# Letting ready large products go ahead of small ones in a planned TensorE order

## The chip, the core and the metric

The kernel runs on one core of a Trainium2 chip. The metric is the device time of one execution in microseconds (us): the median of several runs. Lower is better. TensorE (PE) multiplies, VectorE (DVE), ScalarE (ACT) and GpSimd (POOL) do the element work, SyncE (SP) and the other queues start DMAs. PE's clock has two levels, 1.2 and 2.4 GHz; the profile gives the granted clock as 0.50 or 1.00.

## The reference

```python
def _attn_ref(q, k, v, beta):                       # 4 x 8 heads, 768 tokens, 48 wide
    k_n = k / (norm(k) + 1e-06)
    state = 0                                       # 48 x 48 for each head
    for t in range(768):
        y[t] = q[t] @ state
        state = state + beta[t] * outer(k_n[t], v[t] - k_n[t] @ state)
    return y

x = attn_out as 3072 tokens x 384
h = x @ w_in;  x = (h * sigmoid(1.702 * h)) @ w_out          # 384 -> 2048 -> 384
h = relu(x @ w2_in);  out = (h * h) @ w2_out                 # 384 -> 2048 -> 384
```

## The kernel before

The recurrence is cut into 12 chunks of 64 tokens. Inside a chunk a triangular system is solved (loops on POOL over tiles `U` and `gu`, transposes on DVE), and the chunks follow one another through the state in `ws`. Two chunks give the 512 columns of one tile of the first feed-forward layer, so that this layer starts when chunk 0 is done and runs while the next chunks are computed. The second layer follows, with no small products in it.

PE does two kinds of work here:

- **Large products.** A *group* is three matmuls that follow each other (high by high, high by low, low by high half of an exact split): an *h group* multiplies one third of `x` by a slice of the weights `wi` into PSUM tile `h`; a *z group* multiplies the activated slice `ghi`/`glo` by `wo` into one of three PSUM tiles `z`. Step f of a tile (f = 0 to 15) has three h groups and, later, three z groups. In the first tile steps 0 to 7 are done in two halves of 256 columns, half a (chunk 0) and half b (chunk 1); all other groups are 512 columns wide. Also large: *A* (`a<-kq`, 64x128 x8, the Gram matrices of a chunk) and *Y* (`a<-pqa,ws` and `a<-pqb,ws`, the chunk's output).
- **Small products** of the recurrence: *merge* (`a<-Td,G` and `a<-kT_sb`, 32x16 x64), *W* (`a<-v_sb,Td`, 32x48 x16), *G* (`a<-ws,G`), *S* (`a<-ws,k_sb`, the new state), *X* (`a<-ws,kT_sb`, the state times the keys).

The chain of a chunk is X, subtraction from `v_sb` on DVE, transposes, merge, `Td` on DVE, W, copy to `ws` on ACT, G, subtraction on DVE, W, copy, Y and S, and then X of the next chunk.

The order on every engine is written by a planner, the class `Program`, before the kernel runs. Each operation is added with its queue (or a choice of queues), costs and the tiles it reads and writes; its place in the source, less or more an offset, is its *rank*. `flush` then steps through a time of its own: of the engine that is free first it takes the ready operation with the lowest rank (`n = r[0][1]`, r being a heap of the ready ones), unless an urgent one is due soon, and issues it. Engines work strictly through what is issued to them in this order. A matmul operation carries `cold`, a pair of its cost at the low clock and a count of columns, which the helper `mms` (L275 is its matmul line) sets from a density: 1.0 for groups and A, 0.65 for Y, 0.1 to 0.33 for the small products.

The weights of both layers come as 64-bit floats and are split into two halves for exact products: `split_w` does this on ACT and DVE, and its last subtraction (to `wi_lo` or `wo_lo`) goes to POOL or DVE, whichever the planner has free.

Of the kernel before, what the change touches and what calls it, by code (L numbers as in the profile page):

```python
# [29 lines left out]
TUNE = dict(  # L30
    fused=4,
    warm=(10, 6),
    blocks=(0, 1, 2, 3),
    ja=4,
    depth=2,
    half=8,
    slack=0.0,
    first=2,
# [11 lines left out]
class Program:  # L50
# [8 lines left out]
    def __init__(self, queues):  # L59
        self.queues = queues  # L60
        self.ops = []
        self.writer, self.readers = {}, {}
        self.free = {q: 0.0 for q in queues}
        self.dma_free = 0.0
        self.urgent = False
        self.columns = {}

    def add(self, queue, cost, fn, reads=(), writes=(), early=0, nbytes=0, after=(), cold=None):
        n = len(self.ops)
        deps = set(after)  # L70
        for k in reads:
            if k in self.writer:
                deps.add(self.writer[k])
        for k in writes:
            if k in self.writer:
                deps.add(self.writer[k])
            deps.update(self.readers.get(k, ()))
        for k in reads:
            self.readers.setdefault(k, []).append(n)
        for k in writes:  # L80
            self.writer[k], self.readers[k] = n, []
        queue = (queue,) if isinstance(queue, str) else queue
        cost = cost if isinstance(cost, tuple) else (cost,)
        self.ops.append([queue, cost, fn, deps, n - early, nbytes, None, self.urgent, cold])

    def flush(self):
        left, users, todo = {}, {}, 0
        future = {q: [] for q in self.queues}
        ready = {q: [] for q in self.queues}
        ops = self.ops  # L90

        def arrive(n):
            queue, cost, fn, deps, rank, nbytes, end, urgent, cold = ops[n]
            t = max([ops[d][6] + (self.OWN_LATENCY if ops[d][0] == queue else self.LATENCY) for d in deps], default=0.0)
            for q in queue:
                heapq.heappush(future[q], (t, rank, n))

        for n, op in enumerate(ops):
            if op[6] is None:
                todo += 1  # L100
                wait = [d for d in op[3] if ops[d][6] is None]
                left[n] = len(wait)
                for d in wait:
                    users.setdefault(d, []).append(n)
        for n in left:
            if not left[n]:
                arrive(n)
        done = set()
        while todo:
            best = None  # L110
            for q in self.queues:
                f, r = future[q], ready[q]
                while r and r[0][1] in done:
                    heapq.heappop(r)
                while f and f[0][2] in done:
                    heapq.heappop(f)
                if r or f:
                    t = self.free[q] if r else max(self.free[q], f[0][0])
                    if best is None or t < best[0]:
                        best = (t, q)  # L120
            t, q = best
            f, r = future[q], ready[q]
            while f and f[0][0] <= t:
                x = heapq.heappop(f)
                heapq.heappush(r, (x[1], x[2]))
            while r[0][1] in done:
                heapq.heappop(r)
                if not r:
                    break
            if not r:  # L130
                continue
            n = r[0][1]
            queue, cost, fn, deps, rank, nbytes, end, urgent, cold = ops[n]
            c = cost[queue.index(q)]
            if cold:
                tick = t // self.TICK
                if self.columns.get(tick - 1, 0) < self.WARM_COLUMNS:
                    c = cold[0]
            if not urgent:
                soon = min((x[0] for x in f if ops[x[2]][7] and x[1] < rank and x[2] not in done), default=None)  # L140
                if soon is not None and soon < t + c - TUNE["slack"]:
                    self.free[q] = soon
                    continue
            heapq.heappop(r)
            if cold:
                self.columns[tick] = self.columns.get(tick, 0) + cold[1]
            self.free[q] = t + c
            if nbytes:
                start = max(t + self.DMA_START, self.dma_free)
                self.dma_free = start + nbytes / self.DMA_RATE  # L150
                ops[n][6] = self.dma_free + self.DMA_END
            else:
                ops[n][6] = t + c
            done.add(n)
            todo -= 1
            fn(self.queues[q])
            for u in users.get(n, ()):
                left[u] -= 1
                if not left[u]:
                    arrive(u)  # L160
# [798 lines left out]
```

## Time and profile before

| | |
|---|---|
| median of 3 runs | 1097.75 us (1096.6 to 1100.5) |
| the profiled execution | 1099.22 us, of it 1097.5 us from the first to the last instruction |
| PE busy | 1045.0 us, 95% |
| DVE, ACT, POOL busy | 590.7, 529.8, 339.3 us |
| mean granted clock | 0.960 |
| first tile's steps | about 60 to 222 us of the span |

How to read the rows further down: in the page's strip of 40 slices each digit is a tenth, and 9 is 90% or more. A row of windows has the stretch, then busy time and number of instructions of PE, of the weight loads PEld, of DVE, ACT and POOL, then the granted clock, the share of DMA time and GB/s. A row of the timeline has start, duration, engine, line, operation, tiles, form, count, and in brackets the idle time before it with what ended it. Matmuls overlap in the pipeline, so that the time a group takes is read from the start of its first matmul to the start of what follows, not from the durations. An fp32 matmul of the small kind shows as two records (x32 for 16).

### The profile page before, as it was taken

What the parts mean: (1) busy time and instruction counts of PE and PEld (TensorE: products, weight loads), DVE (VectorE), ACT (ScalarE), POOL (GpSimd) and SP (SyncE); (2) the same over time, 40 slices, a digit from 0 to 9 for tenths busy, and PEclk for the clock granted to TensorE, in tenths of its full rate; (3) what the DMA queues carried; (4) which work ended last, traced back from release to release, by engine and by line L of the source; (5) the groups of instructions that cost most, each with busy time, mean ns of one, the idle gap of its engine ahead of it and who ended that gap; (6) DMA issues with size and microseconds to landing.
All of it is one profiled execution on the core that took longest, in us unless ns stands there. A gap on an engine that the chain in (4) does not pass through costs nothing.

```text
span 1097.5 us, 23999 instructions
## 1 busy us (share of the span) xinstructions
PE 1045.0 (95%) x9900; PEld 847.5 (77%) x9900; DVE 590.7 (54%) x1116; ACT 529.8 (48%) x1088; POOL 339.3 (31%) x679
## 2 busy tenths in 40 slices
PE   5789898989999999999999989999999999999998
PEld 3788787767768776777787866788888888888886
DVE  6788765673636455554644599734333343333332
ACT  4676656555454546454633656633334343333323
POOL 1355351568655573738280044200000000000000
PEclk7688868999999999999999999999999999999999
DMA  7365442223122213222110466401001010000000
GB/s 226 94 180 155 119 130 80 73 69 92 37 76 66 75 41 93 70 69 63 59 34 1 135 176 169 129 1 30 29 1 58 1 58 1 1 30 1 30 1 29
DMA packets 43981, 76.32 MB, mean 70 GB/s; under 512 B 6624, under 2 KB 19552, under 8 KB 43872
## 3 DMA queue, kind: packets, MB, share of 16 engines
q1 hardware_dynamic: 43776, 74.75, 23.1%
q8 instruction: 77, 1.26, 0.5%
q14 instruction: 32, 0.26, 0.1%
q10 hardware_dynamic: 96, 0.05, 0.0%
HBM read 64.16 MB, written 9.44 MB: 67 GB/s over the span
## 4 chain that ended last, share of the span: by engine, by line
PE 68%; DVE 15%; ACT 7%; issue 4%; POOL 4%; DMA 2%; ACTq 0%; SPq 0%; DVEq 0%; POOLq 0%
PE h L275 29%; PE z L275 28%; PE a L275 11%; DVE c L262 3%; ACT G L248 2%; DVE kT_sb L268 2%; DVE glo L258 2%; DVE g L265 1%; DVE c L265 1%; DVE gu L268 1%; POOL tmpp L519 1%; POOL U L522 1%; DMA raw<-in_w_out 1%; DVE v_sb L258 1%; ACT gu L243 1%
## 5 line engine op out<-in xcount | busy, mean ns | idle before, releaser
L243 ACT ACTIVATE g<-h 128x512 f32<-128x512 f32 (+1 forms) x200 | 115.8, 580 | 272.7 <-PE h L275 270.1
L275 PE MATMUL z<-glo,wo_hi 128*128 128x512 f32 (+1 forms) x600 | 233.0, 388 | 6.6 <-DVE glo L258 6.4
L275 PE MATMUL z<-ghi,wo_hi 128*128 128x512 f32 (+1 forms) x600 | 233.1, 388 | 0.6 <-ACT ghi L243 0.5
L275 PE MATMUL z<-ghi,wo_lo 128*128 128x512 f32 (+1 forms) x600 | 230.5, 384 | 0.0
L258 DVE TENSOR_TENSOR glo<-g,ghi 128x512 fp32r<-128x512 f32 (+1 forms) x200 | 137.2, 686 | 102.6 <-ACT ghi L243 102.0
L243 ACT ACTIVATE ghi<-g 128x512 fp32r<-128x512 f32 (+1 forms) x200 | 122.5, 614 | 132.6 <-DVE g L265 65.8
L258 DVE TENSOR_TENSOR g<-g,h 128x512 f32<-128x512 f32 x96 | 66.0, 688 | 172.3 <-ACT g L243 172.2
L275 PE MATMUL h<-x_hi,wi_hi 128*128 128x512 f32 (+1 forms) x312 | 133.5, 428 | 11.0 <-DVE g L265 7.8
L275 PEld LDWEIGHTS z<-glo,wo_hi 128*128 128x128 f32 x600 | 114.7, 191 | 35.8 <-DVE glo L258 14.1
L519 POOL TENSOR_TENSOR tmpp<-U,gu 128x126 f32<-128x126 f32 (+22 forms) x248 | 110.2, 445 | 93.7 <-DVE U L262 75.0
L275 PEld LDWEIGHTS z<-ghi,wo_hi 128*128 128x128 f32 x600 | 114.7, 191 | 25.0 <-ACT ghi L243 1.7
L275 PEld LDWEIGHTS z<-ghi,wo_lo 128*128 128x128 f32 x600 | 114.7, 191 | 21.4
L275 PE MATMUL h<-x_lo,wi_hi 128*128 128x512 f32 (+1 forms) x312 | 122.0, 391 | 3.7 <-DVE x_lo L258 3.6
L265 DVE SCALAR_TENSOR_TENSOR g<-g,h 128x512 f32<-128x512 f32 (+1 forms) x104 | 66.5, 640 | 104.5 <-ACT g L243 104.2
L275 PE MATMUL h<-x_hi,wi_lo 128*128 128x512 f32 (+1 forms) x312 | 121.0, 388 | 0.0
L275 PE MATMUL h<-x_hi,vi_hi 128*128 128x512 f32 x288 | 112.2, 390 | 0.8 <-PE h L275 0.8
L275 PE MATMUL h<-x_hi,vi_lo 128*128 128x512 f32 x288 | 112.1, 389 | 0.0
L522 POOL TENSOR_TENSOR U<-U,tmpp 128x126 f32<-128x126 f32 (+22 forms) x248 | 104.9, 423 | 21.2 <-DVE U L262 2.0
L275 PEld LDWEIGHTS h<-x_hi,wi_hi 128*128 128x128 f32 x312 | 61.5, 197 | 35.3 <-DVE g L265 16.3
L275 PEld LDWEIGHTS h<-x_lo,wi_hi 128*128 128x128 f32 x312 | 62.3, 200 | 12.7 <-DVE x_lo L258 6.0
L275 PEld LDWEIGHTS h<-x_hi,wi_lo 128*128 128x128 f32 x312 | 62.4, 200 | 11.2
L262 DVE TENSOR_SCALAR c<-raw 128x384 uint16<-128x384 uint16 x128 | 64.8, 545 | 5.9 <-DMA raw<-in_w_in 2.9
(117 smaller groups left out, 1457.6 us busy)
## 6 DMA issues: line engine op xcount, KB each, us to landing
raw<-in_w_in SPq DMA_DIRECT2D x32, 384.0 KB, 3.7
raw<-in_w_out SPq DMA_DIRECT2D x32, 384.0 KB, 3.5
kq<-in_kq SPq DMA_DIRECT2D x44, 256.0 KB, 3.0
kT_sb<-in_kq SPq DMA_DIRECT2D x11, 512.0 KB, 4.2
k_sb<-in_kt SPq DMA_DIRECT2D x12, 384.0 KB, 4.3
v_sb<-in_vt SPq DMA_DIRECT2D x12, 384.0 KB, 3.1
xf_sb<-zd SPq DMA_DIRECT2D x18, 256.0 KB, 2.7
out<-zs SPq DMA_DIRECT2D x18, 256.0 KB, 2.0
```

The source lines that it names most:

```text
L243: pg.add("act", c_act(n), lambda e: e.activation(**kw), reads, writes, early)
L248: e.activation(out=out, in_=in_, func=AF.Copy)
L258: pg.add(queue, cost, lambda e: e.tensor_tensor(out=out, in0=in0, in1=in1, op=op), reads, writes, early)
L262: pg.add("dve", c_dve(n, True), lambda e: e.tensor_scalar(**kw), reads, writes, early)
L265: pg.add("dve", c_dve(n), lambda e: e.scalar_tensor_tensor(**kw), reads, writes, early)
L268: pg.add("dve", c_dve(n), lambda e: e.transpose(out=out, in_=in_), reads, writes)
L275: e.matmul(out=out, lhsT=lhsT, rhs=rhs, start=start, stop=stop)
L519: e.tensor_tensor(out=t, in0=U[:, lo:hi, j:j + 1].to_broadcast(shape), in1=gu[:, j + 1:, j:j + 1].rearrange("p i o -> p o i").to_broadcast ...
L522: e.tensor_tensor(out=U[:, lo:hi, j + 1:], in0=U[:, lo:hi, j + 1:], in1=t, op=ALU.add)
```

## The change

`Program` gets a second way to choose on PE. When the lowest-ranked ready operation is small, the planner's time is at most 220, and 6 us of it have passed since the last long row of large products ended, the ready large operation of the lowest rank is taken instead. A row counts as long when large operations have followed each other without a gap for 4 us of planned time.

```diff
+    burst=(6, 4, 220),
...
+        self.run = self.run_end = self.burst_end = 0.0
...
+    def large(self, n):
+        cost, cold = self.ops[n][1], self.ops[n][8]
+        return cold is None or cold[1] > 1400 * cost[0]
+
+    def large_first(self, r, t, done):
+
+        pause, length, until = TUNE["burst"]
+        if t > until or t < self.burst_end + pause or self.large(r[0][1]):
+            return 0
+        ready = [(x, k) for k, x in enumerate(r) if x[1] not in done and self.large(x[1])]
+        return min(ready)[1] if ready else 0
...
-            n = r[0][1]
+            k = self.large_first(r, t, done) if q == "pe" else 0
+            n = r[k][1]
...
-            if not urgent:
+            if not urgent and not k:
...
-            heapq.heappop(r)
+            if k:
+                r[k] = r[-1]
+                r.pop()
+                heapq.heapify(r)
+            else:
+                heapq.heappop(r)
+            if q == "pe":
+                self.run = (self.run if self.large(n) and t < self.run_end + 0.3 else 0.0) + (c if self.large(n) else 0.0)
+                self.run_end = t + c
+                if self.run >= TUNE["burst"][1]:
+                    self.burst_end = t + c
```

No instruction is added or dropped. The order is the same up to the merge that the trace of before shows at 77.75 us, and PE's is the same again from 558 us. Lines after the class stand 25 lower, so that the matmul line L275 is L300 in the changed kernel. What moves is seen at three places on PE.

First, the second merge of chunk 1 (`a_74<-kT_sb`), in step 5 of half a. Before, it stands right behind the first h group of the step, then A and both W, then large groups:

```order
L275 MATMUL h_68<-x_hi_80,wi_hi 128x256
L275 MATMUL h_68<-x_lo_81,wi_hi 128x256
L275 MATMUL h_68<-x_hi_80,wi_lo 128x256
L275 MATMUL a_74<-kT_sb 32x16 x64
L275 MATMUL a_73<-kq_100 64x128 x8
L275 MATMUL a_74<-v_sb,Td_112 32x48 x16
L275 MATMUL a_72<-v_sb,Td_112 32x48 x16
L275 MATMUL h_68<-x_hi_80,wi_hi 128x256
```

In the change the same merge follows A and five groups, of which these are the last two, and the first W comes one h group later:

```order
L300 MATMUL z_70<-ghi_84,wo_hi 128x256
L300 MATMUL z_70<-glo_86,wo_hi 128x256
L300 MATMUL z_70<-ghi_84,wo_lo 128x256
L300 MATMUL z_71<-ghi_84,wo_hi 128x256
L300 MATMUL z_71<-glo_86,wo_hi 128x256
L300 MATMUL z_71<-ghi_84,wo_lo 128x256
L300 MATMUL a_74<-kT_sb 32x16 x64
L300 MATMUL h_67<-x_hi_80,wi_hi 128x256
L300 MATMUL h_67<-x_lo_81,wi_hi 128x256
L300 MATMUL h_67<-x_hi_80,wi_lo 128x256
L300 MATMUL a_74<-v_sb,Td_112 32x48 x16
```

So merge and A have changed places, five groups have gone ahead of the merge, and the second W (`a_72`) comes after five groups more. Further on in this chunk the first h group of step 7 has moved ahead of the third W.

Second, chunk 2 after its merges, in steps 4 to 8 of half b. Before, two W stand after three groups, then two groups, a G, a group, a G, and so on:

```order
L275 MATMUL z_69<-ghi_84,wo_hi 128x256
L275 MATMUL z_69<-glo_86,wo_hi 128x256
L275 MATMUL z_69<-ghi_84,wo_lo 128x256
L275 MATMUL a_74<-v_sb,Td_111 32x48 x16
L275 MATMUL a_72<-v_sb,Td_111 32x48 x16
L275 MATMUL h_67<-x_hi_80,wi_hi 128x256
L275 MATMUL h_67<-x_lo_81,wi_hi 128x256
L275 MATMUL h_67<-x_hi_80,wi_lo 128x256
L275 MATMUL z_70<-ghi_84,wo_hi 128x256
L275 MATMUL z_70<-glo_86,wo_hi 128x256
L275 MATMUL z_70<-ghi_84,wo_lo 128x256
L275 MATMUL a_73<-ws_95,G_105 32x48
```

In the change eleven groups stand in one row between the merge and the first W. These are the last two, and what follows them:

```order
L300 MATMUL h_68<-x_hi_80,wi_hi 128x256
L300 MATMUL h_68<-x_lo_81,wi_hi 128x256
L300 MATMUL h_68<-x_hi_80,wi_lo 128x256
L300 MATMUL z_71<-ghi_84,wo_hi 128x256
L300 MATMUL z_71<-glo_86,wo_hi 128x256
L300 MATMUL z_71<-ghi_84,wo_lo 128x256
L300 MATMUL a_74<-v_sb,Td_111 32x48 x16
L300 MATMUL h_67<-x_hi_80,wi_hi 128x512
L300 MATMUL h_67<-x_lo_81,wi_hi 128x512
L300 MATMUL h_67<-x_hi_80,wi_lo 128x512
L300 MATMUL a_72<-v_sb,Td_111 32x48 x16
```

The W and G of chunk 2 have moved 10 to 14 operations back; behind the second W follow six more groups before the first G.

Third, A and the merges of chunk 3, in steps 10 and 11. Before, both stand ahead of the last h group of step 10 and all z groups of step 9:

```order
L275 MATMUL a_73<-kq_99 64x128 x8
L275 MATMUL a_74<-Td_112,G_106 32x16 x64
L275 MATMUL h_67<-x_hi_80,wi_hi 128x512
L275 MATMUL h_67<-x_lo_81,wi_hi 128x512
L275 MATMUL h_67<-x_hi_80,wi_lo 128x512
L275 MATMUL z_69<-ghi_85,wo_hi 128x512
```

In the change that h group and the three z groups come first, and one h group of step 11 stands between A and the merge:

```order
L300 MATMUL z_71<-ghi_85,wo_hi 128x512
L300 MATMUL z_71<-glo_87,wo_hi 128x512
L300 MATMUL z_71<-ghi_85,wo_lo 128x512
L300 MATMUL a_73<-kq_99 64x128 x8
L300 MATMUL h_68<-x_hi_80,wi_hi 128x512
L300 MATMUL h_68<-x_lo_81,wi_hi 128x512
L300 MATMUL h_68<-x_hi_80,wi_lo 128x512
L300 MATMUL a_74<-Td_112,G_106 32x16 x64
```

So five groups have gone ahead of the merge. The planner's time shifts with all this, and so the other engines' orders change too: among others, six subtractions to `wi_lo` and `wo_lo` go from POOL to DVE.

## Rows read from the trace of the kernel before

**Rows 1.** The page, granted clock of PE in 40 slices.

```profile
PEclk7688868999999999999999999999999999999999
```

**Rows 2.** Windows, cut where the granted clock changes.

```profile
core 0: us, PE busy (x) PEld busy (x) DVE busy (x) ACT busy (x) POOL busy (x), PEclk, DMA share, GB/s
...
82.10:88.90 6.80, 6.01 (x70) 5.70 (x65) 5.19 (x11) 4.02 (x11) 2.28 (x2) 0.50 0.54 174
...
106.00:109.40 3.40, 3.40 (x17) 3.40 (x18) 3.22 (x8) 2.23 (x7) 2.83 (x7) 0.50 1.03 333
...
123.00:126.50 3.50, 3.27 (x17) 2.98 (x16) 3.50 (x9) 0.84 (x3) 0.00 (x0) 0.51 0.42 112
...
133.30:153.80 20.50, 20.50 (x290) 18.57 (x290) 12.10 (x30) 9.45 (x22) 8.78 (x21) 0.50 0.41 115
...
170.80:177.70 6.90, 5.74 (x148) 4.44 (x144) 4.35 (x7) 3.55 (x9) 0.53 (x1) 0.51 0.16 42
177.70:230.00 52.30, 52.30 (x761) 42.20 (x761) 27.43 (x52) 32.67 (x76) 26.91 (x55) 1.00 0.30 90
230.00:242.00 12.00, 9.12 (x38) 6.31 (x37) 11.59 (x25) 4.29 (x7) 6.10 (x13) 1.00 0.01 1
```

**Rows 3.** Timeline of PE, in the stretch at the low clock.

```profile
140.91 1.49 PE L275 MATMUL a<-ws,G 32*32 32x48 f32 x32
142.33 0.58 PE L275 MATMUL z<-ghi,wo_hi 128*128 128x256 f32 x1
...
143.13 0.41 PE L275 MATMUL h<-x_hi,wi_hi 128*128 128x256 f32 x1
...
143.77 0.41 PE L275 MATMUL z<-ghi,wo_hi 128*128 128x256 f32 x1
...
145.19 1.49 PE L275 MATMUL a<-v_sb,Td 32*32 32x48 f32 x32
146.61 0.58 PE L275 MATMUL h<-x_hi,wi_hi 128*128 128x256 f32 x1
...
150.54 0.34 PE L275 MATMUL a<-pqa,ws 128*48 128x64 f32 x1
...
153.99 0.50 PE L275 MATMUL h<-x_hi,wi_hi 128*128 128x512 f32 x1
```

**Rows 4.** Timeline of PE, the same kinds at the full clock.

```profile
89.83 1.55 PE L275 MATMUL a<-ws,G 32*32 32x48 f32 x64
...
92.25 0.28 PE L275 MATMUL z<-ghi,wo_hi 128*128 128x256 f32 x1
...
92.61 0.28 PE L275 MATMUL z<-ghi,wo_hi 128*128 128x256 f32 x1
...
93.42 0.87 PE L275 MATMUL a<-v_sb,Td 32*32 32x48 f32 x32
94.22 0.39 PE L275 MATMUL z<-ghi,wo_hi 128*128 128x256 f32 x1
...
94.68 0.28 PE L275 MATMUL z<-ghi,wo_hi 128*128 128x256 f32 x1
...
96.05 0.26 PE L275 MATMUL a<-pqa,ws 128*48 128x64 f32 x1
...
98.41 0.39 PE L275 MATMUL h<-x_hi,wi_hi 128*128 128x256 f32 x1
```

**Rows 5.** Timeline of PE, A and first merge of chunk 3.

```profile
170.41 1.61 PE L275 MATMUL a<-kq 64*64 64x128 f32 x16 [2.16 <-DVE v_sb L258]
173.19 1.90 PE L275 MATMUL a<-Td,G 32*32 32x16 f32 x128 [1.16 <-DVE Td L258]
175.02 0.80 PE L275 MATMUL h<-x_hi,wi_hi 128*128 128x512 f32 x1
...
176.47 0.63 PE L275 MATMUL z<-ghi,wo_hi 128*128 128x512 f32 x1
```

**Rows 6.** Timeline of POOL, low half of step 7's `wi`.

```profile
95.95 1.16 POOL L258 TENSOR_TENSOR wi_lo<-c,wi_hi 128x384 fp32r<-128x384 f32 x1 [4.79 <-ACT wi_hi L243]
```

## The prediction

> **What bounds the kernel now.** PE is busy for 95% of the span, so I looked first for where its time is dear, and that is the strip of the granted clock on the page [rows 1]: from the eighth slice on it shows nines, and the sevens, sixes and eights stand in the first seven, about 190 us. The change begins at 77.75 us, so I then cut windows at the places where the clock changes [rows 2]. From there on there are five stretches at 0.50 up to 178 us: 6.8, 3.4, 3.5, 20.5 and 6.9 us, 41 us together. After them PE runs at 1.00 for 52.30 us without a pause.
>
> The fourth of them is the one to look at. PE is busy for 20.50 of 20.50 us in it, and still the clock stays at its low level: 1.2 GHz. The timeline shows what PE does there [rows 3]: a W or G of 32 records, one to four groups, another W or G, and so on until both Y. The second and third stretch are the counterpart: 17 records in 3.4 and 3.5 us [rows 2], groups of large matmuls alone with no small product between them, and both end with the clock back at 1.00. So in this trace the two low stretches of nothing but large products ended after five or six groups each, and the one broken up by small products went on for 20 us.
>
> What PE pays for that is read by setting the two timelines side by side. At the low clock W takes 1.42 us (145.19 to 146.61), G 1.42 (140.91 to 142.33), both Y 3.45 (150.54 to 153.99), a group 0.64 (143.13 to 143.77), and 0.80 when it is the first behind a small product [rows 3]. At the full clock W takes 0.80 (93.42 to 94.22), G half of 1.55, both Y 2.36 (96.05 to 98.41), a group 0.36 (92.25 to 92.61), and 0.46 behind a small product (94.22 to 94.68) [rows 4].
>
> After 178 us PE has no idle time for 52 us, so what is won or lost before then goes through to the end, unless a wait on the recurrence takes it. The first such place is 230 to 242 us, with 2.9 us of idle PE and DVE busy for 11.59 of 12.00 us [rows 2].
>
> **The change part by part.** The instructions are the same, so the sum is made of clock, idle time and waits.
>
> *Second place (133 to 154 us).* In the low stretch stand four W, two G, both Y and eleven groups, by the order shown. At the full clock they would take 4 x 0.80 + 2 x 0.78 + 2.36 + 11 x 0.40 = 11.5 us, 0.40 being between a group in a row and one behind a small product. Against 20.5 us that is 9.0 us. The change puts the eleven groups in a row ahead of the first W. If the clock falls at the same time as before, by the second and third stretch some five of them run at 0.64 instead of 0.36, which leaves 5 x 0.28 = 1.4 us unsaved, and if it stays low for all eleven, 3.1 us. Behind them W, G and Y alternate with groups of 512 columns, and that is the kind of mix that keeps 1.00 after 177.7 us. I take 7.5 us of gain, with 5.9 and 9.0 as ends.
>
> *Third place (168 to 178 us).* PE waits 2.16 us for `v_sb` ahead of A and 1.16 us for `Td` ahead of the merge [rows 5], 3.3 us together, while an h group and z groups stand behind the merge in PE's order and start without a wait of their own once it is through. The change puts five groups ahead of that merge. A group of 512 columns at the full clock I estimate at twice that of 256 less the restart, 0.70 us: five are 3.5 us and fill the whole idle time. The low stretch from 170.8 us goes with it if PE stays busy: the h group took 1.45 us (175.02 to 176.47) instead of 0.70, the z group behind it and the merge (1.83) about 0.7 each over the full-clock time, A 0.5 by its 1.61 us: some 2.5 us. So the ends are 0 and 5.8 us. I take 3.0, the middle, because the X products that feed `v_sb` and `Td` come one or two places later too.
>
> *First place (77 to 89 us).* Five groups run ahead of the merge, while the clock is still full; before, three of them ran in the first low stretch at 0.64, so 3 x 0.28 = 0.8 us are saved. If the row keeps the clock up altogether, the stretch of 6.8 us, half of it groups and half W, gives 2.4 us with the ratios above. Against it stands that the merge comes five groups and an A later, 5 x 0.36 + 1.0 = 2.8 us, and the chain of chunk 1 with it; but the W that waited behind the merge was followed by those same groups, so the G gets its place back. I take 0.5 us of gain, between a gain of 2.4 and a loss of 2.8.
>
> *Large products that are not ready.* A group that goes ahead of a small product holds it back when its own operands are late. The clearest case is step 7 of half a, whose first h group now stands ahead of the third W of chunk 1. In the trace the low half of its weights lands at 95.95 + 1.16 = 97.1 us [rows 6], and that W ran at 93.42 [rows 4]. If the weights come no earlier, W starts at 97.1 + 0.36 at best, 4.0 us late, with G's result, the second W, Y and S queued behind it on PE, and ACT's copies and the DMA of the next half's `x` behind those. The wait on POOL was for `wi_hi` from ACT, 4.79 us [rows 6], and the order puts that conversion two places earlier on ACT, ahead of the copies of W. So I take 2.0 us, between 0 and 4.0. The z groups of step 6 of half b stand ahead of the first G of chunk 2 in the same way; there I count nothing, because the groups that they depend on have moved up by more.
>
> *The other engines.* Six subtractions of the weight split go from POOL, 1.16 us each [rows 6], to DVE. Together that is less than 7 us, and in the low stretch DVE has 8.4 us idle of 20.5 [rows 2], so I cost it at nothing; if that cover is gone, as it is from 230 us, DVE's 0.4 us of idle there would not hold one of them.
>
> *After 178 us.* At 1.00 and with no idle time there is nothing to win, while small products stand up to nine places later until the rule ends. The chain can bear that while there are groups to run; the place where it can't is 230 to 242 us. I take 0.5 us of loss, between 0 and another 2.9 us like that idle time.
>
> Sum: 7.5 + 3.0 + 0.5 - 2.0 - 0.5 = 8.5 us less. Against its own time of 1099.2 us (a span of 1097.5 and 1.7 around it) the profiled execution would take 1090.7. It was 1.5 us above the median, so the median goes from 1097.75 to **1089.3 us**.
>
> The page "TensorE: Matmul & The Clock Gate" of the Trainium skill, section "Why this matters for your kernels", tells kernel authors that what costs clock in mid-kernel are idle gaps of PE between bursts of matmuls. By that rule a stretch without gaps has nothing to win from a new order, and the time would stay at 1097.75. The stretch of 20.50 busy us at 0.50 [rows 2] disagrees with it, so I give it a small chance below. That the clock is a thing of two levels, as the same page has it (Part 1), the rows agree with: 0.50 and 1.00 and, at the edges, 0.51.
>
> **The rivals.**
>
> *Given back to the recurrence: no change.* The clock rises, but W, G, Y and S of chunk 2 come later by the groups put ahead of them, and the merge of chunk 3, which already waits for `Td` at 173.19 [rows 5], comes no earlier than before. Then the second place gives nothing and only the fill at the third remains, 3.0 us, less the 2.0 and 0.5 above: 1097 us. For it speaks that wait. Against it speaks the stretch before: in 133 to 154 us PE never waited [rows 2], so the chain waited for PE and gets shorter with it.
>
> *The row does not lift the clock: no change.* The groups stand together, but the low stretch starts where it did and goes on. Then 1097 to 1099 us. Against it are the second and third stretch. Idle gaps as the only cause (above) end in the same time.
>
> *The recurrence is the bound and is held back: slower.* Ten groups more stand ahead of the first W of chunk 2. At 0.36 to 0.64 us they make it 3.6 to 6.4 us late. If what lies between this W and the merge of chunk 3 (134 to 173 us) is bound by ACT, DVE and POOL and not by PE, everything behind comes that much later, and groups pulled forward are missing to fill it: 1097.75 + 5 = about 1103 us. It decides when of these 39 us less than the delay was time in which the chain waited for PE. PE's full 20.50 us [rows 2] speaks against it, DVE's 12.10 busy us there too.
>
> **How the numbers follow.** A measurement of this kernel tells 0.3%, 3.3 us, from no change. Chances: the forecast, from 1083 to 1094.4 us, 0.63; more than that, the upper ends of the second and third place together (9.0 + 5.8 + 2.4 = 17 us, 1080.6), 0.05; given back, 0.14; the clock not lifted by a row 0.04, idle gaps alone 0.02; held back, 0.12. So faster 0.68, same 0.20, slower 0.12. The range from 1081 to 1099.5 us leaves out the slower case, the upper edge of no change, and little below; the forecast's own range is 1083 to 1094.4.
>
> **What would show it.** In the changed kernel's windows the low clock between 77 and 178 us should come to some 15 to 25 us instead of 41, and the long stretch should be under 11 us and begin with groups alone. Y of chunk 2, at 150.54 us before, should not be later; the merge of chunk 3 should come before 169 us, with the idle time ahead of it under 2 us. The end of the first tile should be 7 to 10 us earlier, and stay so to the end of the span. A wait of PE for `wi_lo` (from POOL) ahead of a W near 90 to 97 us would show the stall of step 7. I am wrong if the long stretch is only moved to another place, or if the idle time of PE between 77 and 178 us has grown by what the clock gave.

## The result and the profile after

The changed kernel takes 1083.01 us, the median of four executions from 1081.6 to 1085.8, against 1097.8 us before: a ratio of 0.9864 with an interval of [0.9847, 0.9881]. Measured again later, on the chip of all the runs below but the last, it took 1086.2 us (1084.08 to 1087.95) against 1098.39, a ratio of 0.9888 [0.9868, 0.9907]. So it is 12 to 15 us faster; the forecast was 8.5 us.

The strip of the granted clock of the changed kernel now has its last low digit in the fourth slice:

```profile
PEclk7798999999999999999999999999999999999999
```

Its windows, cut where the clock changes and then at round places, with the columns of [rows 2]:

```profile
84.30:91.20 6.90, 6.65 (x87) 6.09 (x89) 4.78 (x20) 2.32 (x5) 0.00 (x0) 0.51 0.55 146
...
101.40:104.80 3.40, 3.40 (x80) 3.25 (x78) 2.13 (x4) 3.30 (x9) 2.90 (x7) 0.50 0.42 135
...
128.70:132.10 3.40, 3.40 (x49) 3.18 (x49) 3.40 (x13) 1.97 (x6) 1.15 (x2) 0.50 0.22 21
132.10:153.00 20.90, 20.90 (x439) 17.98 (x431) 18.41 (x45) 13.51 (x31) 13.12 (x32) 1.00 0.60 167
153.00:170.00 17.00, 15.45 (x344) 11.56 (x346) 14.57 (x26) 11.26 (x25) 3.80 (x4) 1.00 0.38 112
170.00:221.00 51.00, 49.24 (x720) 39.20 (x714) 27.71 (x55) 32.06 (x75) 26.41 (x52) 1.00 0.31 92
221.00:233.00 12.00, 10.39 (x43) 7.93 (x43) 10.80 (x24) 4.62 (x8) 10.19 (x26) 1.00 0.01 1
...
282.00:400.00 118.00, 114.83 (x1445) 91.99 (x1440) 62.38 (x115) 61.63 (x132) 74.80 (x162) 1.00 0.23 66
```

Read it against [rows 2]. Low clock between 76 and 178 us is 13.7 us instead of 41; I had expected 15 to 25. Of the stretches of 3.5 and 20.50 us around the merges of chunk 2 one of 3.40 is left, and the 20.90 us behind it are at 1.00 with PE just as full. That one stands earlier in the order than the stretch of 20.50 did: it covers most of a row of five groups between the two merges of chunk 2 (128.38 to 131.61 us; three groups in before) and ends inside the second merge, ahead of the row of eleven. Nothing lies low at the third place any more.

The timeline of PE at the second place, which answers to [rows 3]:

```profile
131.61 2.00 PE L300 MATMUL a<-kT_sb 16*32 16x16 f32 x128
133.54 0.39 PE L300 MATMUL h<-x_hi,wi_hi 128*128 128x256 f32 x1
...
137.24 0.28 PE L300 MATMUL z<-ghi,wo_hi 128*128 128x256 f32 x1
137.68 0.87 PE L300 MATMUL a<-v_sb,Td 32*32 32x48 f32 x32
138.48 0.50 PE L300 MATMUL h<-x_hi,wi_hi 128*128 128x512 f32 x1
...
142.82 0.87 PE L300 MATMUL a<-ws,G 32*32 32x48 f32 x32
143.62 0.50 PE L300 MATMUL h<-x_hi,wi_hi 128*128 128x512 f32 x1
...
149.29 0.26 PE L300 MATMUL a<-pqa,ws 128*48 128x64 f32 x1
...
151.22 0.39 PE L300 MATMUL z<-ghi,wo_hi 128*128 128x256 f32 x1
```

From 133.54 the row of groups runs at 0.36 a piece, W and G take 0.80 (137.68 to 138.48, 142.82 to 143.62) instead of 1.42, and both Y 1.93 instead of 3.45. Y stands at 149.29 instead of 150.54, with six groups of 512 columns done ahead of it that came later before.

A and the first merge of chunk 3, which answer to [rows 5]:

```profile
164.01 1.09 PE L300 MATMUL a<-kq 64*64 64x128 f32 x16
165.03 0.50 PE L300 MATMUL h<-x_hi,wi_hi 128*128 128x512 f32 x1
166.60 1.26 PE L300 MATMUL a<-Td,G 32*32 32x16 f32 x128 [0.61 <-DVE Td L283]
167.79 0.50 PE L300 MATMUL h<-x_hi,wi_hi 128*128 128x512 f32 x1
```

The wait ahead of A is gone, that ahead of the merge is 0.61 us instead of 1.16, and the merge stands at 166.60 instead of 173.19. The row that answers to [rows 6], the low half of step 7's weights in the timeline of POOL:

```profile
93.42 1.02 POOL L283 TENSOR_TENSOR wi_lo<-c,wi_hi 128x384 fp32r<-128x384 f32 x1 [9.44 <-ACT wi_hi L268]
```

And the waits of PE from 76 to 170 us (total, times, longest):

```profile
PE h L300 <- DVE g L290: 3.4, 3, 1.5
PE a L300 <- ACT ws L273: 1.9, 3, 1.5
...
PE h L300 <- DVE wi_lo L283: 0.4, 1, 0.4
```

The weights of step 7 are there at 94.4 us instead of 97.1, in time for the group ahead of the third W, which starts at 94.90. The stall that I feared is not there; the only wait for `wi_lo` is one of 0.4 us, for a half that DVE makes.

### The profile page after: what moved, and what is told of

Read it like the earlier page. It is cut to its first block, busy times and chain, and to the rows that moved or that the text cites. A ratio compares the mean times of both kernels' runs of the same rounds, so it can differ in the third digit from the quotient of the medians.

```text
span 1082.7 us, 23994 instructions
## 1 busy us (share of the span) xinstructions
PE 1024.4 (95%) x9900; PEld 832.9 (77%) x9900; DVE 589.6 (54%) x1122; ACT 528.5 (49%) x1088; POOL 332.9 (31%) x673
## 4 chain that ended last, share of the span: by engine, by line
PE 66%; DVE 16%; ACT 8%; issue 4%; POOL 3%; DMA 2%; SPq 1%; DVEq 0%; ACTq 0%; POOLq 0%
PE h L300 28%; PE z L300 28%; PE a L300 9%; DVE c L287 3%; ACT G L273 3%; DVE kT_sb L293 2%; DVE glo L283 2%; DVE c L290 2%; DVE gu L293 1%; DVE g L290 1%; POOL tmpp L544 1%; DVE v_sb L283 1%; POOL U L547 1%; ACT gu L268 1%; DVE x_lo L283 1%
## 5 line engine op out<-in xcount | busy, mean ns | idle before, releaser
L300 PE MATMUL z<-glo,wo_hi 128*128 128x512 f32 (+1 forms) x600 | 231.8, 386 | 5.6 <-DVE glo L283 5.6
L300 PE MATMUL z<-ghi,wo_hi 128*128 128x512 f32 (+1 forms) x600 | 232.0, 387 | 0.1
L300 PE MATMUL z<-ghi,wo_lo 128*128 128x512 f32 (+1 forms) x600 | 229.7, 383 | 0.0
L300 PE MATMUL h<-x_hi,wi_hi 128*128 128x512 f32 (+1 forms) x312 | 129.9, 416 | 18.3 <-DVE g L290 15.1
L544 POOL TENSOR_TENSOR tmpp<-U,gu 128x126 f32<-128x126 f32 (+22 forms) x248 | 113.2, 457 | 95.8 <-DVE U L287 77.0
L300 PEld LDWEIGHTS z<-glo,wo_hi 128*128 128x128 f32 x600 | 113.7, 189 | 33.2 <-DVE glo L283 11.8
L300 PEld LDWEIGHTS z<-ghi,wo_hi 128*128 128x128 f32 x600 | 113.6, 189 | 24.0 <-ACT ghi L268 0.9
L300 PEld LDWEIGHTS z<-ghi,wo_lo 128*128 128x128 f32 x600 | 113.7, 190 | 21.5
L300 PE MATMUL h<-x_lo,wi_hi 128*128 128x512 f32 (+1 forms) x312 | 118.8, 381 | 3.2 <-DVE x_lo L283 3.2
L300 PE MATMUL h<-x_hi,wi_lo 128*128 128x512 f32 (+1 forms) x312 | 118.7, 380 | 0.4 <-DVE wi_lo L283 0.4
L300 PE MATMUL h<-x_hi,vi_hi 128*128 128x512 f32 x288 | 112.4, 390 | 0.8 <-PE h L300 0.8
L300 PE MATMUL h<-x_hi,vi_lo 128*128 128x512 f32 x288 | 112.2, 390 | 0.0
L547 POOL TENSOR_TENSOR U<-U,tmpp 128x126 f32<-128x126 f32 (+22 forms) x248 | 102.8, 415 | 20.4 <-DVE U L287 1.3
L300 PEld LDWEIGHTS h<-x_hi,wi_hi 128*128 128x128 f32 x312 | 59.7, 191 | 42.3 <-DVE g L290 24.7
L300 PEld LDWEIGHTS h<-x_hi,wi_lo 128*128 128x128 f32 x312 | 60.0, 192 | 11.6 <-DVE wi_lo L283 0.6
L300 PEld LDWEIGHTS h<-x_lo,wi_hi 128*128 128x128 f32 x312 | 60.1, 192 | 11.2 <-DVE x_lo L283 4.4
L273 ACT ACTIVATE ws<-a 32x384 f32<-32x384 f32 x92 | 44.3, 482 | 49.6 <-PE a L300 45.2
```

What stands on the lines that cost most here:

```text
L273: e.activation(out=out, in_=in_, func=AF.Copy)
L300: e.matmul(out=out, lhsT=lhsT, rhs=rhs, start=start, stop=stop)
L544: e.tensor_tensor(out=t, in0=U[:, lo:hi, j:j + 1].to_broadcast(shape), in1=gu[:, j + 1:, j:j + 1].rearrange("p i o -> p o i").to_broadcast ...
L547: e.tensor_tensor(out=U[:, lo:hi, j + 1:], in0=U[:, lo:hi, j + 1:], in1=t, op=ALU.add)
```

## Where the lead comes from

To place the gain I took matmuls that stand at the same place in PE's order in both kernels, behind the same operations, and the time from one to the next. Their starts in before are 75.29 (first merge of chunk 1), 122.49 (h group), 163.84 (z group of step 8), 223.20 (A, behind the first tile), 271.87 (h group), 290.48 (G), 404.20 (Y) and 515.13 us (h group); in the change 76.26, 122.49, 155.07, 212.30, 261.19, 281.64, 390.94 and 500.45. Each column is one profiled execution; a star marks a stretch that has the order of the change. The last six are experiments, told below.

| stretch in before | before | change | change again | to 394 | to 261 | first tile | third | second | later |
|---|---|---|---|---|---|---|---|---|---|
| 75 to 122, first place | 47.2 | 46.2* | 46.1* | 45.5* | 46.9* | 50.9* | 46.9 | 48.2 | 47.2 |
| 122 to 164, second | 41.4 | 32.6* | 32.9* | 33.0* | 33.1* | 33.4* | 38.7 | 35.4* | 41.1 |
| 164 to 223, third | 59.4 | 57.2* | 58.8* | 57.1* | 57.5* | 58.1* | 54.9* | 62.9 | 59.3 |
| 223 to 272 | 48.7 | 48.9* | 48.8* | 49.4* | 49.2* | 58.0 | 58.1 | 48.3 | 48.1* |
| 272 to 290 | 18.6 | 20.5* | 20.5* | 20.4* | 21.1 | 18.6 | 18.6 | 18.6 | 20.5* |
| 290 to 404 | 113.7 | 109.3* | 109.3* | 109.3* | 113.5 | 114.2 | 114.1 | 114.1 | 110.7* |
| 404 to 515 | 110.9 | 109.5* | 110.2* | 113.0 | 110.6 | 110.8 | 110.5 | 110.5 | 109.5* |

In the change's first column the gains are 1.0 at the first place, 8.8 at the second, 2.1 at the third, then -0.2, -1.8, +4.4 and +1.4 us. It started 1.0 us late, at the merge where the orders are still the same.

## The experiments

**Parts of the rule.** The rule is limited to a stretch of the planner's time, or asks for a shorter row. `since` is a new lower bound.

```diff
-    burst=(6, 4, 220),
+    burst=(6, 4, 100),               # e1_first
+    burst=(6, 4, 122), since=100,    # e2_second
+    burst=(6, 1.5, 220),             # e8_short15
-        if t > until or t < self.burst_end + pause or self.large(r[0][1]):
+        if t > until or t < TUNE["since"] or t < self.burst_end + pause or self.large(r[0][1]):
```

First place alone:

> The rule works only up to 100 of the planner's time, that is at the first place alone; at the second place small products break the groups up after at most four. Theory A: the long low stretch is there again, over 10 us of it, and the time is 1094 to 1099 us. Rival B (each place gives its part): about 1091 us.

Measured: 1092.6 us (1089.81 to 1100.43, eight executions), ratio 0.9943 [0.9918, 0.9968]. The spread is over 10 us, and the median lies between the two theories, so it decides for neither. In its profile (an execution of 1098.15 us, the second slowest) the long stretch of the second place stands as before, 20.4 us at 0.50. The four quickest (1089.81 to 1090.78 us) have a mean granted clock of 0.972 to 0.976 against 0.964 there; where they were less low is not in a trace. As in the next run, the planner's later choices shift too.

Second place alone:

> The rule works only between 100 and 122 of the planner's time, so that the order is that of before up to the second merge of chunk 2 and has the row of eleven groups behind it. Theory A (what the change gives is the clock at this one place; the other places give little): the long low stretch is gone and the time is 1083 to 1088 us, and not above the change's 1083 by more than 5, since the first place cost the changed kernel 1.8 us. Rival B (the gain is a sum over all the bursts): 1089 to 1092 us.

Measured: 1088.95 us (1086.56 to 1090.6), ratio 0.9897 [0.9878, 0.9916]. About 11 us, against 12 to 15 for the change, and between the two theories. But the planner's later choices shift with it, so this is not the second place alone, as the cuts below show.

A row that counts as long after 1.5 us instead of 4:

> The rule as in the change, but a row counts as long after 1.5 us of planned time instead of 4, so that at the second place five groups follow the merge and then small products stand between one to three groups. Theory A (the length of the row is what lifts the clock): a low stretch of over 10 us stays and the time is 1092 to 1098 us. Rival C (ready groups ahead of waiting small products fill PE, whatever the clock does): 1084 to 1088 us.

Measured: 1092.33 us (1090.31 to 1094.78), ratio 0.9931 [0.9912, 0.9949]; its profile still has 13.7 us at 0.50 from 124.5 us. So it is 5 us behind the change. Whether the shorter rows are the cause is not told by it, since the planner's later choices shift here too, and p4_second below, with the long row, also shows 13.7 us at this place in its profile.

**A row of large products without a new order.** The order of before stays as it is on all engines; behind the second merge of chunk 2 come eleven groups more, with weights of zero, which add nothing to `z`.

```diff
...
+        if n == 2:
+            second = len(pg.ops) - 1
+            for i in range(11):
+                def idle_group(e, i=i):
+                    for rhs in (x_hi[0], x_lo[0], x_hi[0]):
+                        e.matmul(out=z_ps[i % KX][:, CT:], lhsT=zw_sb, rhs=rhs[:, i % KX, CT:], start=False, stop=False)
+                pg.add("pe", 0.0, idle_group, [], [], 0, 0, [second])
...
```

> The kernel before, its order unchanged, with eleven added groups of 256 columns behind the second merge of chunk 2; their weights are zero and they add zero to z, so that they are work for nothing. Theory A (a row of large products lifts the clock, and the clock is what is worth the time): the row costs 5 to 7 us, the work behind it falls from 20.5 to about 11.5 us, and the time is 1092 to 1096 us, faster than before in spite of the added work. Rival C (the gain comes from where the groups stand and not from the clock): 5 to 7 us slower than before, 1102 to 1105 us.

Measured: 1099.73 us (1096.5 to 1101.06), ratio 1.0005 [0.9991, 1.0019]. The end missed what I expected, but the windows show what the row does:

```profile
132.50:135.90 3.40, 3.40 (x18) 3.40 (x17) 3.40 (x12) 0.44 (x2) 1.52 (x4) 0.50 0.73 238
135.90:153.00 17.10, 17.10 (x328) 15.48 (x327) 10.41 (x21) 10.38 (x24) 9.31 (x19) 1.00 0.41 124
...
170.00:180.30 10.30, 10.16 (x294) 8.80 (x294) 3.44 (x7) 4.17 (x11) 0.53 (x1) 0.50 0.29 79
```

The low stretch at this place is 3.4 us instead of 20.5, and the same W, G and groups that stayed low before now run at 1.00. The added row itself took 5.3 us (132.76 to 138.09 in the timeline), and still A of chunk 3 started at 167.35 instead of 170.41. So the row lifts the clock: shown by itself, with nothing else moved. Without the row the low stretch was 20.5 us long in before and in p1_late (below), and 13.6 in p3_third. And it is not this one profile alone: the ten executions have a mean granted clock of 0.966 (0.962 to 0.970), the seventeen of before measured with them 0.961, which I estimate at 11 us less at 0.50 in an execution (0.005 of 1098 us, doubled, because a stretch at 0.50 lowers the mean by half of its length). Behind it the lead is lost: PE waits 1.9 us for `v_sb` and 1.7 for `Td` there, and the low stretch at the third place is 10.3 us instead of 6.9.

**One order spliced to the other.** In the next seven kernels the planner makes both plans, with the rule and without, and the operations are issued by the one up to a time of its plan and by the other from there on. The cuts stand where PE has done the same operations in both plans, so that a stretch has, on PE, exactly the order of one kernel.

```diff
+        orders = {}
+        for rule in (1, 0):
...
+            self.off = not rule
+            orders[rule] = self.order()
+        done = set()
+        for rule, until in TUNE["parts"]:
+            for t, q, n in orders[rule]:
+                if t < until and n not in done:
+                    done.add(n)
+                    self.ops[n][2](self.queues[q])
...
+    parts=((0, 173.1), (1, 9e9)),                  # p1_late
+    parts=((1, 172.5), (0, 9e9)),                  # p2_early
+    parts=((0, 122.5), (1, 172.5), (0, 9e9)),      # p3_third
+    parts=((0, 95.9), (1, 123.9), (0, 9e9)),       # p4_second
+    parts=((1, 212.6), (0, 9e9)),                  # p6_to290
+    parts=((0, 95.9), (1, 9e9)),                   # p7_not_first
+    parts=((1, 329.0), (0, 9e9)),                  # p8_to394
```

The order behind the first tile alone ("later" in the table):

> Every engine follows the order of before up to the end of the first tile (about 222 us of its span) and the order of the change from there on. In the trace of the change the lead over before grew by about 5 us after 290 us, where before has two stretches at 0.50 (3.5 and 3.4 us near 328 and 386 us) and the change has none. Theory 1, the order behind the first tile has a gain of its own: 4 to 6 us less than before (1092 to 1095 us), with no stretch at 0.50 between 315 and 400 us. Theory 2, the lead grew because the recurrence came out of the first tile earlier: same as before within 1 us, and the two stretches stay. The time between the start and the end of the first tile is that of before under both.

Measured: 1095.13 us (1093.38 to 1096.54), ratio 0.9956 [0.9942, 0.9969], 4.8 us less. Theory 1 holds for the time: the later order has a gain of its own, which nothing before 222 us caused. One of the two stretches at 0.50 is still there (328.7 to 332.2 us), the other is gone.

The first tile alone:

> The mirror image: the order of the change up to the end of the first tile, then that of before. Theory 1 (the later order has its own gain): 9 to 11 us less than before (1087 to 1090 us), the stretches at 0.50 near 317 and 375 us are there. Theory 2 (the lead grows by itself): about 15 us less (1083 us), without these stretches.

Measured: 1098.82 us (1093.38 to 1104.13, twelve executions), ratio 0.9987 [0.9971, 1.0002]. Neither theory: a kernel with all three places of the change, and before's order behind them, wins next to nothing. Its profile (the slowest of the twelve, which need not all look like it: the mean clock is 0.958 here and 0.973 in the quickest) has two long stretches at 0.50 that the change has not:

```profile
86.80:103.90 17.10, 17.10 (x255) 15.43 (x254) 10.80 (x31) 8.88 (x21) 7.34 (x20) 0.50 0.38 117
...
234.00:237.00 3.00, 0.47 (x1) 0.19 (x1) 1.00 (x1) 2.33 (x4) 0.98 (x3) 1.00 0.00 0
237.00:254.10 17.10, 15.52 (x178) 11.31 (x177) 7.15 (x13) 4.75 (x9) 11.44 (x29) 0.50 0.11 32
```

The second of them begins right behind idle time. PE's timeline there:

```profile
236.53 0.51 PE L320 MATMUL z<-ghi,wo_hi 128*128 128x512 f32 x1 [2.57 <-ACT ghi L288]
...
239.77 2.77 PE L320 MATMUL a<-v_sb,Td 32*32 32x48 f32 x64
242.47 0.80 PE L320 MATMUL z<-ghi,wo_hi 128*128 128x512 f32 x1
...
244.05 1.49 PE L320 MATMUL a<-ws,G 32*32 32x48 f32 x32
245.47 0.80 PE L320 MATMUL z<-ghi,wo_hi 128*128 128x512 f32 x1
```

This is the mix of the second place again, small products broken up by single groups, and it stays at 0.50 in the same way. What PE waited for is seen on ACT:

```profile
234.63 1.33 ACT L288 ACTIVATE gu<-U,dup_sb 128x512 f32<-128x512 f32 x2 [5.96 <-POOL U L567]
235.87 0.61 ACT L288 ACTIVATE ghi<-g 128x512 fp32r<-128x512 f32 x1
```

`ghi`, which the group needs, stands behind the copy of `gu` on ACT, and that waits 5.96 us for the triangular solve on POOL. PE has come early to a place where the recurrence has not. In the table the stretch from 223 to 272 us takes 58.0 us instead of 48.7, and that uses up the lead.

The third place alone:

> Only the third place has the order of the change (from the end of chunk 2 to the end of the first tile); ahead of it and behind it the order is that of before, with the long stretch at 0.50. My theory, that this place is worth its idle time and its clock by itself: 2 to 4 us less than before, the idle time ahead of A and the merge of chunk 3 under 1.5 us instead of 3.3, the stretch of 6.9 us at 0.50 from 170.8 us shorter or gone. Rival, that it only matters once the second place is quicker: within 1 us of before.

Measured: 1104.39 us (1100.3 to 1106.55, twelve executions), ratio 1.0037 [1.0021, 1.0053]: slower. At its own place it does more than I asked: 54.9 us instead of 59.4, at 1.00 from 160 to 231 us and without the waits. Then the lead is lost at the same later place, with the same 17.1 us, so this loss is not only that of a slowest execution:

```profile
231.00:233.90 2.90, 1.08 (x5) 0.52 (x3) 0.82 (x1) 2.18 (x4) 1.05 (x4) 1.00 0.00 0
233.90:251.00 17.10, 15.56 (x178) 11.31 (x177) 7.38 (x13) 4.90 (x10) 11.29 (x28) 0.50 0.09 32
```

The profile is of an execution of 1100.79 us, one of its quicker ones; what the ones above 1105 us lose more is not in a trace. Nor is it all gain of the order up to 223 us: the second place, in before's order here, happened to be low for 13.6 us and not 20.5.

The second place alone:

> Only the second place has the order of the change (the eleven groups ahead of the first W of chunk 2, and the mix behind them, to the end of chunk 2); ahead and behind the order is that of before. Theory 1, the places add up: 6 to 9 us less than before, the long stretch under 5 us. Rival, given back at the third place for want of the groups that fill it there: the lead is 7 to 9 us at the second Y of chunk 2 and falls to under 4 us by the end of the first tile, with more than 3.3 us of idle time ahead of A and the merge of chunk 3; then 0 to 4 us less than before at the end.

Measured: 1095.34 us (1093.31 to 1098.23), ratio 0.996 [0.9945, 0.9974]; 4.4 us less, between the two theories. In its profile (1098.23, its slowest) the rival is what happens: the second place gains 5.9 us, and the third, with before's order, gives 3.5 back. PE's timeline there:

```profile
168.61 1.97 PE L320 MATMUL a<-kq 64*64 64x128 f32 x16 [3.34 <-DVE v_sb L303]
171.40 1.90 PE L320 MATMUL a<-Td,G 32*32 32x16 f32 x128 [0.82 <-DVE Td L303]
```

Against [rows 5] the idle time is 4.2 us instead of 3.3, and the low stretch around it 10.2 us (166.1 to 176.3).

The change's order up to 261 us, then before's:

> The change's order up to 261 us of its span (272 us of before), then that of before: against the run whose cut is at the end of the first tile, only the 50 us behind the first tile are different. There, with before's order, PE waited 2.57 us for ghi ahead of the W of chunk 4 and went through 17 us at 0.50. Theory, these 50 us decide whether the lead is kept: 1084 to 1089 us, no long stretch at 0.50 behind 212 us, but the two short ones of before near 317 and 375 us. Rival, the order behind 261 us is what keeps it: 1094 to 1101 us as in that run.

Measured: 1091.5 us (1089.99 to 1093.03), ratio 0.9939 [0.9922, 0.9956]. 50 us of order more than p2_early, and 5 us less by the ratios; the stretch from 223 to 272 us takes 49.2 us, with no low clock. The time lies between the two bands, 2.5 us above that of the theory and as far below the rival's. In its main point the theory holds: with these 50 us the lead is kept through them. Behind them 5.3 us are still missing against the change.

The change without its first place:

> The order of before up to 122 us of the span, that of the change from there on: the change without its first place. If the first place cost 1.8 us in the change's profile, as the shift of A of chunk 2 says, and adds spread: 1081 to 1085 us. If its row is worth something for what follows: 1086 to 1092 us.

Measured: 1086.91 us (1084.35 to 1091.24), ratio 0.9903 [0.9879, 0.9926], against 0.9888 [0.9868, 0.9907] for the change itself in the same runs:

> The change itself once more, on the chip of the other runs. In the run with the change's order up to the end of the first tile, the same order of the first place went through 17 us at 0.50 (86.8 to 103.9 us) where the change's own profile shows 6.9 (84.3 to 91.2): the fall came 2.5 us later against the same instructions. If the change's time hangs on where the fall comes, its executions spread over 6 us or more (1081 to 1092 us), and this profile may show the long stretch at the first place. If the four times of the change (1081.6 to 1085.8 us) are all there is, they stay within 5 us.

The first place is worth nothing that can be told. The change's nine executions lie between 1081.6 and 1087.95 us, so its own time does not jump by 6 us on one chip; the first place was low for 6.9 us in one profile and 3.5 in the other.

The change's order up to 394 us, then before's:

> The change's order up to 394 us of its span (408 us of before), then that of before. The run with the cut at 261 us was at 1091.5 us, the change on the same chip at 1086.2: 5.3 us lie behind 261 us. Between 261 and 394 us stand the two places where before and that run have a stretch at 0.50 (320 to 324 and 378 to 382 us there). Theory, the two places are the 5 us, since small products stand together there in the change's order and idle time comes ahead of groups: 1085 to 1088 us, no stretch at 0.50 between 310 and 390 us. Rival, the gain is spread over what comes behind 394 us too: 1088.5 to 1091.5 us.

Measured: 1088.67 us (1086.66 to 1090.16), ratio 0.9908 [0.989, 0.9925]; on another chip, so only the ratios are compared. From p6_to290 to this ratio are 3.4 us, from this to the change 2.2, where the intervals overlap. Between 261 and 394 us lies most, not all, of what I was missing, just over the theory's band; as the rival had it, something lies behind too (110.9 against 109.5 us in the last row of the table, with no low clock in either, and 113.0 where the orders are spliced). In its profile 310 to 390 us are at 1.00.

What is different there is seen by setting the run p6_to290, which has before's order at this place, against the change. Its timeline of PE around the second of the two low stretches (378.1 to 381.5 us):

```profile
376.05 0.87 PE L320 MATMUL a<-v_sb,Td 32*32 32x48 f32 x32 [1.40 <-DVE Td L303]
376.84 0.50 PE L320 MATMUL h<-x_hi,wi_hi 128*128 128x512 f32 x1
...
379.49 0.63 PE L320 MATMUL h<-x_hi,wi_hi 128*128 128x512 f32 x1
```

And the change, measured again, at the same step:

```profile
374.38 0.50 PE L300 MATMUL h<-x_hi,wi_hi 128*128 128x512 f32 x1 [1.32 <-DVE g L290]
375.19 0.39 PE L300 MATMUL h<-x_hi,wi_hi 128*128 128x512 f32 x1
...
378.69 1.55 PE L300 MATMUL a<-v_sb,Td 32*32 32x48 f32 x64
380.17 0.50 PE L300 MATMUL h<-x_hi,wi_hi 128*128 128x512 f32 x1
```

The long wait is nearly the same. In the one it stands ahead of a W, two groups follow, with a second wait of 0.44 us for `glo` in the last of them, and the clock goes low; in the other it stands ahead of groups, both W come together behind them, and the clock stays. That the order makes the difference is what this pair suggests; no run has it alone.

## Why the prediction was right, and by how much it was short

The direction and the mechanism were right. What the sum priced came out close: at the G of 290.48 us the change is 8.8 us ahead, against 8.5 for the sum. The rest of the lead in this profile, 5.8 us, comes behind that and was not priced; with it the first median, 1083.01 us, stands at the very edge of the forecast's range (from 1083). That it stayed inside is luck. Point by point:

- *Second place, 7.5 us (5.9 to 9.0).* It measured 8.8 us in the change, and 8.0 to 8.5 in the other four executions with all of the change's first tile; 5.9 in p4_second, where the clock fell earlier in the order and stayed low through the row of five. In the change the clock was back when the row of eleven began (132.1 and 133.54 us), so none of the 1.4 to 3.1 us that I took off for it was paid in that row, and it is not the eleven that lifted it there; the mix behind them keeps 1.00. The second profile of the change has the same (back at 130.8, row from 133.10 us). In p8_to394, p6_to290 and p2_early, with the same order, it went as I had assumed: the clock fell within 1.2 us of the row's start and came back inside the row, 3.4 us later, and in p8_to394 the eleven took 5.6 us (130.58 to 136.22) instead of 4.1. That a row brings the clock back is also shown by the added zero groups. Both Y took 1.93 us at the full clock, not the 2.36 that I had read.
- *Third place, 3.0 us (0 to 5.8).* It measured 2.1 us (0.6 to 2.3 in the others). No clock was low there, but PE still waits 2.2 us in this stretch instead of 3.3, now for `g`, `ws`, `Td` and `glo`, 0.7 us at most each. In the second run of the change 171.8 to 175.2 us are low, which goes with its 0.6.
- *First place, +0.5, and products that are not ready, -2.0.* The two together measured +1.0 us in the change, -3.7 to +1.7 in the others. The stall of step 7 did not come, because the conversion that had moved up on ACT brought the weights 2.7 us earlier; I had taken the middle of its bounds, and the end at nothing was right. The 2.4 us that I gave as the upper end of the place should have been 2.6, by 6.01 busy us and the ratios; the sum does not use it. Measured as a whole, by p7_not_first, the place is worth nothing.
- *After 178 us, -0.5 (0 to -2.9).* This is the step that was mis-sized. At the end of the rule, 223 to 290 us, the loss is 2.0 us, inside the bounds. But behind it the change won 5.8 us (4.4 + 1.4), which is borne out by p1_late (4.8 us, with that loss in it) and by p6_to290 against the change (5.3 us). I wrote that at 1.00 there is nothing to win and took that from 52 us of [rows 2] for the rest of the kernel. The trace of before has two stretches at 0.50 further on, 327.8 to 331.3 and 385.9 to 389.3 us, which the strip of tenths shows as nines. The rule itself does nothing there, being past its limit; the planner's time is different by then and its choices come out differently. That gain is a by-product.
- *The rivals.* "Given back to the recurrence" is not what the change does, but it is what parts of it do: the zero row and p4_second give back at the third place, p2_early and p3_third at 237 and 234 us. The price is larger than I had it, since the wait does not only use up the lead but takes the clock with it; in p3_third the end is slower than before. The change escapes because its order runs on past the first tile: PE's idle time there, 2.2 us for `g`, stands ahead of a row of groups, and the clock did not fall. In p7_not_first, with the same order there, it did fall behind the same wait, at 220.1 us, but inside the row, and it was back after 3.4 us (223.5) and not after 17.1.
- *Idle gaps as the cause of the low clock.* Behind 178 us each of the falls in these profiles comes where PE had just been idle: 0.47 us busy in the 3.00 us ahead of 237.0. On that side the trace goes with the page "TensorE: Matmul & The Clock Gate" of the Trainium skill, section "Why this matters for your kernels", which blames gaps between bursts, though the gap here, 2.57 us, is shorter than those that it warns of. At the second place the traces do not agree with it: in p8_to394 the clock fell at 130.7 and in e1_first at 132.4 us with PE busy for all of the 3.00 us before. The windows of p8_to394:

```profile
127.70:130.70 3.00, 3.00 (x137) 2.79 (x136) 3.00 (x11) 2.03 (x6) 3.00 (x2) 1.00 0.46 123
130.70:134.10 3.40, 3.40 (x17) 3.40 (x18) 3.40 (x12) 0.38 (x1) 1.12 (x4) 0.50 0.59 170
```

Most of that time is the second merge of chunk 2 (128.47 to 130.58 us). Nor do they agree on the length: once low, 15.5 of 17.1 us were busy and still low, and the 20.50 us of [rows 2] ended when a row was put into them, with no gap taken out. So gaps are not all that tells where it falls; that small products without a gap do it too is suggested by the place of the merge and not tested. How long it lasts goes with the order and, as the last section shows, with where in it the fall comes.

What stays open: why p1_late keeps the stretch at 328.7 us with the change's order, and why p7_not_first has one of 6.8 us (315.7 to 322.5) at the same place. So the order alone does not fix a fall there. Open, too, is where the 1.4 us in the last row of the table come from, since neither its clock nor its idle time is different.

## What to carry to other kernels

Where small products are broken up by single large ones, look at the clock of that stretch before its idle time: a row of ready large products put ahead of them paid 8 us at its place here, with no instruction saved. Price such a gain to the next place where the engine waits on another chain, because a lead that runs into a wait ahead of small products is lost there, clock and all: the three places together were worth 1.4 us without the 50 us of order behind them, and 12 to 15 with the rest. And cut windows over the whole span: a strip of tenths hid two low stretches of 3.4 us.

## What was not expected of the hardware

The same order of instructions meets the low clock at different instructions in different executions. At the first place, with the change's order, it was low for 6.9 us in the change's profile, 3.5 in the second one, 3.4 in p6_to290, 17.1 in p2_early, and not at all in p8_to394:

```profile
75.00:110.30 35.30, 29.25 (x723) 25.67 (x725) 31.53 (x80) 26.04 (x64) 16.32 (x35) 1.00 0.58 170
```

In the change the fall came at 84.3 us, ahead of a row of five groups (86.48 to 89.98), and the clock was back at 91.2. In p2_early it came at 86.8, inside the same row (85.77 to 88.47); W, G and short rows followed, and it stayed low until 103.9 us. At the second place p4_second fell at 125.1, stayed low through five groups between the merges (130.69 to 134.19), and came back at 138.8, inside the long row that starts at 136.13. So what a row is worth depends on where the fall comes, and executions of one kernel can lie 10 us apart, as those of e1_first and p2_early do; the change's own nine lie within 6.4 us.
